# Weight sums for the last block's seven products made beside the first stages of blocks 2 to 4, with the last block's first and last group reordered

## The chip, the core and the metric

The kernel runs on one core of a Trainium2 chip. The engines work side by side, each through its own instructions in order: PE (TensorE, matmuls), PEld (the weight loads of TensorE), DVE (VectorE), ACT (ScalarE), POOL (GpSimd) and SP, which here only issues DMA transfers. The metric is the device time in microseconds (us) of one execution; lower is better.

## What is computed

Three layers over 4 x 768 = 3072 tokens of width 512, all in fp32:

```python
state = gamma * state + k_t^T v_t ; y_t = scale * q_t @ state     # retention, 8 heads of 64
xn = x / rms(x) * rms_g                                           # layer 2
x  = (silu(xn @ w_gate) * (xn @ w_val)) @ w_out                   # d_ff = 1536
h  = x @ w_in ; solu = h * softmax(h)                             # layer 3, d_ff = 1024
out = layernorm(solu) * g_ln @ w_out2
```

The weights come as doubles. Each fp32 operand of a matmul is split into a high and a low half, and a product is three matmuls: high by high, low by high, high by low.

## The kernel before

The tokens are worked in six blocks of 512 (0 to 5, `n` in the code). A block has two stages.

**First stage** (`bc_block`): layer 2 in 12 groups `m` of 128 columns of `d_ff` (`g = 12 n + m` counts them through the kernel). A group loads a gate tile and a value tile (tag `w4`, four buffers) and a tile of `w_out` (tag `wo`, two buffers), each with its halves. `gv(g, 0)` and `gv(g, 1)` are the gate and value products, 12 matmuls each into the banks GB and VB; ACT makes the Silu, `act_hl` multiplies on DVE (L613) and splits the product into halves; one group later `cmm` multiplies it by `w_out`, 12 matmuls into the banks X0 to X3. Pieces of the next block's retention (`att_pieces`) lie between: on PE the lines L154 to L185, on POOL `qd` (L144), `kd` (L136) and the state's decay (L198).

**Second stage** (`de_block`): layer 3 on four tiles `t` of 128 tokens. `d_mm` multiplies by `w_in`; DVE finds the mean (L801) and subtracts it from one half of the tile, POOL from the other half (L803); `t_tr` transposes the result on PE (L814), ACT and DVE split it (L102, L103) and `e_mm` multiplies by the second `w_out`. In the same stage `rms_1t`, `rms_2t` and `rms_3` make the next block's normalised tokens: one column sum on PE (L297), a power on POOL (L299), a transpose (L302) and four multiplications (L240, for the last block L319) on DVE. The second stage of block 0 runs behind that of block 1.

**Block 5** (`bc_block7`, since `FROM = 5`) makes the gate and value products of a group, which are two 2 x 2 products of sub-blocks, by seven half-size products instead of eight (`product(i, ...)`, 6 matmuls of 256 columns each). Products 3, 5, 6 and 7 want sums of weight sub-blocks. These are made ahead, once for each of the 12 groups: in the second stages of blocks 1, 2 and 3, four groups each (`SUMS`). `s_fetch(m)` loads a group's gate and value tiles again into the two `wo` buffers, `s_make(m)` adds the halves on POOL (L641, twice) and makes four sums (L643 to L646), and SP stores them to DRAM. In block 5 `s_load` brings a group's sums back (tag `st`, three buffers) and `s_split` makes their halves (ACT casts, L315; POOL subtracts, L316). In a group the order is products 1 and 5, the next group's split, products 6 and 7, `cm(0)` (a quarter of the group before's `w_out` product), 2 and 3, `cm(1, 2)`, product 4, `cm(3)`; at the end `cmm` does the last group's own `w_out` product.

**What sets the order.** `slot(n, s)` runs what is filed under a step `s` of block `n`, `w_slot` the weight loads of a plan: gate and value tiles are asked for two groups ahead. Up to the end of block 4 a scheduler may then move instructions on each engine; behind that (`in_order(mark)`) the order is the written one. SP issues transfers strictly in order, so a store that waits for POOL holds up the loads behind it.

Of the kernel before, what the change touches and what calls it, by code (L numbers as in the profile page):

```python
# [9 lines left out]
F32 = mybir.dt.float32  # L10
F32R = mybir.dt.float32r
# [7 lines left out]
P = 128  # L19
# [15 lines left out]
CHAIN = 12  # L35
W2_AT = [36 + 2 * j for j in range(16)]
FROM = 5
SUMS = {1: (0, 4), 2: (4, 8), 3: (8, 12)}


@with_exitstack
def retention_moe_kernel(ctx: ExitStack, tc: tile.TileContext, qk0, q2, kt, kv, wpk, w2i, w2o,
# [45 lines left out]
    def wt(tag, shape, dt, bufs):  # L88
        cnt[0] += 1
        return wp.tile(shape, dt, tag=tag, name=f"{tag}_{cnt[0]}", bufs=bufs)  # L90

    def st():
        return wt("st", [P, 512], F32, 3)
# [419 lines left out]
    def parts(w, part):  # L513

        return (w[:, :, 0, :], w[:, :, 1, :]) if part < 2 else (w[:, 0, :], w[:, 1, :])
# [74 lines left out]
    def w_slot(s):  # L590
        order = {w_split: 0, w2_fin: 0, w_conv: 1, conv: 1, w_load: 2, load64: 2}
        for f, a in sorted(wsched.pop(s, []), key=lambda x: order[x[0]]):
            f(*a)
# [6 lines left out]

    def gv(g, part):
        w = wsp.pop((g, part))
        halves = [slice(0, 256), slice(256, 512)] if g == 0 else [slice(0, 512)]
        for ts_ in halves:
            for k in range(NK):
                mm3(GV[part][:, ts_], *wk(w, k), xnh[:, k, ts_], xnl[:, k, ts_], k == 0, k == NK - 1)
# [3 lines left out]
    def act_hl(m):  # L610
        silu = acts.pop(("s", m))
        a = silu[:, 1, :]
        nc.vector.tensor_tensor(out=a, in0=GV[1], in1=silu[:, 0, :], op=ALU.mult)  # L613
        ah, al = r2(), r2()
        split(ah, al, a)
        acts[m] = (ah, al)
# [10 lines left out]
    sscr = [[dp.tile([P, 2, 256], F32, tag=f"s{m}_{i}", name=f"s{m}_{i}") for i in range(2)] for m in range(NM)]  # L627
    sums = {}

    def s_fetch(m):  # L630
        for part in range(2):
            w = wt("wo", [P, 2, 2, 256], F32R, 2)
            nc.sync.dma_start(w.bitcast(F32), scr[m][part])
            sums[m, part] = w

    def s_make(m):

        g, v = (parts(sums.pop((m, part)), part) for part in range(2))
        G = nc.gpsimd
        for hi, lo in (g, v):  # L640
            G.tensor_tensor(out=hi.bitcast(F32), in0=hi.bitcast(F32), in1=lo.bitcast(F32), op=ALU.add)  # L641
        g, v = g[0].bitcast(F32), v[0].bitcast(F32)
        G.tensor_tensor(out=v[:, 1], in0=v[:, 0], in1=v[:, 1], op=ALU.add)  # L643
        G.tensor_tensor(out=v[:, 0], in0=g[:, 0], in1=v[:, 0], op=ALU.subtract)
        G.tensor_tensor(out=g[:, 0], in0=v[:, 1], in1=g[:, 0], op=ALU.subtract)
        G.tensor_tensor(out=g[:, 1], in0=g[:, 1], in1=g[:, 0], op=ALU.subtract)  # L646
        nc.sync.dma_start(sscr[m][0], g)
        nc.sync.dma_start(sscr[m][1], v)
# [16 lines left out]
    def product(i, g, ps):  # L665

        if i in (1, 2, 4):
            w = wsp[g, 1 if i == 4 else 0]
            hi, lo = w[:, i != 1, 0, :], w[:, i != 1, 1, :]
        else:  # L670
            a, b = {6: (0, 0), 3: (0, 1), 7: (1, 0), 5: (1, 1)}[i]
            hi, lo = (t[:, a, b, :] for t in shl[g])
        xh, xl = xq(i)
        for k in range(2):
            cs = slice(k * P, k * P + P)
            mm3(ps, hi[:, cs], lo[:, cs], xh[:, k, :], xl[:, k, :], k == 0, k == 1)

    def bc_block7(n):


        base = 3 * NM * n
        V, G = nc.vector, nc.gpsimd
        gb, vb = (t.rearrange("p (h x) -> p h x", h=2) for t in GV)
        for m in range(NM):
            g = n * NM + m
            c = f4()
            cq = c.rearrange("p a (h x) -> p a h x", h=2)
            c11, c12, c21, c22 = (cq[:, a, h, :] for a in range(2) for h in range(2))
            u23 = wt("r2", [P, 2, 256], F32, 8)

            def cm(*ds):
                if m:
                    cmm(g - 1, m - 1, ds)

            def add(eng, out, x, y):
                eng.tensor_tensor(out=out, in0=x, in1=y, op=ALU.add)  # L696

            product(1, g, gb[:, 0])
            product(5, g, gb[:, 1])
            nc.scalar.copy(cq[:, :, 0, :], gb)  # L700
            if m + 1 < NM:
                s_split(g + 1)
            if m + 2 < NM:
                s_load(g + 2)
            w_slot(base + 3 * m)
            slot(n, 3 * m)
            product(6, g, vb[:, 0])
            product(7, g, vb[:, 1])
            add(V, u23[:, 0], vb[:, 0], c11)
            add(V, u23[:, 1], vb[:, 1], u23[:, 0])  # L710
            add(G, c12, u23[:, 0], c21)
            add(G, c22, u23[:, 1], c21)
            cm(0)
            product(2, g, gb[:, 0])
            product(3, g, gb[:, 1])
            slot(n, 3 * m + 1)
            w_slot(base + 3 * m + 1)
            add(V, c[:, 0, :], GV[0], c[:, 0, :])
            nc.scalar.activation(c[:, 0, :], c[:, 0, :], AF.Silu)
            if m == NM - 1 and n and PRE & 2:  # L720
                nc.scalar.activation(wt("sm", [P, 12], F32, 4)[:, 0:1], c[:, 0, 0:1], AF.Exp)
            cm(1, 2)
            product(4, g, vb[:, 0])
            add(V, c21, vb[:, 0], u23[:, 1])
            V.tensor_tensor(out=c[:, 1, :], in0=c[:, 1, :], in1=c[:, 0, :], op=ALU.mult)
            ah, al = r2(), r2()
            split(ah, al, c[:, 1, :])
            acts[m] = (ah, al)
            shl.pop(g)
            slot(n, 3 * m + 2 if m < NM - 1 else 34)  # L730
            cm(3)
            w_slot(base + 3 * m + 2)
        cmm(n * NM + NM - 1, NM - 1)

# [2 lines left out]
    def slot(n, s):  # L737
        for f in extra.pop((max(n, s // 52), s), []):
            f()

    def bc_block(n):
        base = 3 * NM * n
        for m in range(NM):
            g = n * NM + m
            if g == CHAIN:
                chain[0] = False
            with tc.issue_after(m0.ins) if g == 0 else nullcontext():
                gv(g, 0)
            s = f4()
            acts["s", m] = s  # L750
            nc.scalar.activation(s[:, 0, :], GV[0], AF.Silu)  # L751
            if m == NM - 1 and n and PRE & 2:
                nc.scalar.activation(wt("sm", [P, 12], F32, 4)[:, 0:1], s[:, 0, 0:1], AF.Exp)
            slot(n, 3 * m)
            w_slot(base + 3 * m)
            with tc.issue_after(m0.ins) if g == 0 else nullcontext():
                gv(g, 1)
            slot(n, 3 * m + 1)
            act_hl(m)
            w_slot(base + 3 * m + 1)  # L760
            if m:
                cmm(g - 1, m - 1)
            if m < NM - 1:
                slot(n, 3 * m + 2)
            else:
                slot(n, 34)
            w_slot(base + 3 * m + 2)
        cmm(n * NM + NM - 1, NM - 1)
# [247 lines left out]
    for n in range(NB):  # L1016
        if n + 1 < NB:
            if n == 0:
                span, r = 30, (31, 33, 34, 34, 35, 35)
            elif n == 1:  # L1020
                span, r = 45, (47, 49, 51, 53, 55, 57)
            else:
                span, r = 35, (37, 39, 41, 43, 45, 47) if n + 1 < FROM else (37, 39, 41, 42, 43, 44, 45, 46, 47, 48, 49, 50)
            pieces = att_pieces(n + 1)
            for i, f in enumerate(pieces):
                extra.setdefault((n, i * span // (len(pieces) - 1)), []).append(f)
            for s, f in zip(r, rms_steps(SB, n + 1)):
                extra.setdefault((n, s), []).append(f)
        if n == FROM - 1:
            g = FROM * NM  # L1030
            extra.setdefault((n, 45), []).append(lambda: s_load(g))
            extra.setdefault((n, 47), []).append(lambda: (s_split(g), s_load(g + 1)))
        if n in SUMS:
            for i, m in enumerate(range(*SUMS[n])):
                extra.setdefault((n, 36 + 4 * i), []).append(lambda m=m: s_fetch(m))
                extra.setdefault((n, 39 + 4 * i), []).append(lambda m=m: s_make(m))
        (bc_block if n < FROM else bc_block7)(n)
        if n == 0:
            after.close()
            x2_store()  # L1040
            slot(0, 35)
            continue
        de_block(n, XB, 35)
        if n == FROM - 1:
            mark = nc.cur_bb.bb.instructions[-1]
        if n == 1:
            de_block(0, x2_load(), 52)
# [72 lines left out]
```

## Time and profile before

| | |
|---|---|
| median of 3 runs | 1071.24 us (1071.00 to 1072.85) |
| the profiled execution | 1072.65 us |
| its span, first to last instruction | 1070.8 us |
| around the span | 1.85 us |
| PE busy, share of the span | 1034.8 us, 97% |
| mean granted TensorE clock | 0.986 of 2.4 GHz |

The profile is of one execution. Its own time, not the median, belongs to its rows. A matmul of 512 columns starts every 0.23 us at the full clock and every 0.43 us at half of it.

### The profile page before, as it was taken

What the parts mean: (1) busy time and instruction counts of PE and PEld (TensorE: products, weight loads), DVE (VectorE), ACT (ScalarE), POOL (GpSimd) and SP (SyncE); (2) the same over time, 40 slices, a digit from 0 to 9 for tenths busy, and PEclk for the clock granted to TensorE, in tenths of its full rate; (3) what the DMA queues carried; (4) which work ended last, traced back from release to release, by engine and by line L of the source; (5) the groups of instructions that cost most, each with busy time, mean ns of one, the idle gap of its engine ahead of it and who ended that gap; (6) DMA issues with size and microseconds to landing.
All of it is one profiled execution on the core that took longest, in us unless ns stands there. A gap on an engine that the chain in (4) does not pass through costs nothing.

```text
span 1070.8 us, 15022 instructions
## 1 busy us (share of the span) xinstructions
PE 1034.8 (97%) x5390; PEld 826.5 (77%) x5390; DVE 602.3 (56%) x1065; ACT 432.9 (40%) x816; POOL 456.7 (43%) x538
## 2 busy tenths in 40 slices
PE   9999999998999999999989999989999999999998
PEld 7867767776788777777767777767777777899887
DVE  5897877698366642353683343484244458244452
ACT  4556566456235452222353222343222236333333
POOL 6865764677147530121484010177121008455321
PEclk9899999999999999999989999998999999999999
DMA  9699998886645204666526666534665521367301
GB/s 351 203 314 336 304 316 324 272 286 215 236 157 188 99 31 160 213 196 209 178 79 205 199 211 217 189 108 138 212 212 195 171 85 30 121 235 247 108 1 40
DMA packets 73931, 203.18 MB, mean 190 GB/s; under 512 B 8321, under 2 KB 14849, under 8 KB 73857
## 3 DMA queue, kind: packets, MB, share of 16 engines
q1 hardware_dynamic: 65072, 177.05, 49.8%
q10 hardware_dynamic: 8784, 25.17, 5.9%
q8 instruction: 43, 0.70, 0.3%
q14 instruction: 32, 0.25, 0.1%
HBM read 169.68 MB, written 32.51 MB: 189 GB/s over the span
## 4 chain that ended last, share of the span: by engine, by line
PE 65%; DVE 7%; DMA 7%; POOL 6%; issue 3%; ACT 1%; SPq 0%; POOLq 0%; ACTq 0%; DVEq 0%
PE X L597 9%; PE X L598 9%; PE X L599 9%; PE GB L597 6%; PE GB L599 6%; PE GB L598 6%; PE VB L597 5%; PE VB L599 5%; PE VB L598 5%; DMA wo<-scr 4%; DVE st L502 2%; PE YB L174 2%; PE YB L171 1%; PE SB L154 1%; POOL st L501 1%
## 5 line engine op out<-in xcount | busy, mean ns | idle before, releaser
L144 POOL TENSOR_TENSOR qd<-rq,qtab_t 64x256 f32<-64x256 f32 x68 | 61.1, 899 | 189.9 <-PE YB L171 159.9
L598 PE MATMUL X<-r,wo 128*128 128x512 f32 x264 | 105.7, 400 | 0.2 <-DVE r L103 0.2
L599 PE MATMUL X<-r,wo 128*128 128x512 f32 x264 | 105.3, 399 | 0.0
L597 PE MATMUL X<-r,wo 128*128 128x512 f32 x264 | 103.1, 407 | 1.8 <-ACT r L102 1.8
L597 PE MATMUL GB<-xnh,w 128*128 128x512 f32 (+1 forms) x268 | 102.0, 380 | 2.4 <-DVE f L696 2.2
L599 PE MATMUL GB<-xnh,w 128*128 128x512 f32 (+1 forms) x268 | 100.5, 375 | 0.3 <-DVE w L103 0.3
L598 PE MATMUL GB<-xnl,w 128*128 128x512 f32 (+1 forms) x268 | 100.3, 374 | 0.0
L613 DVE TENSOR_TENSOR f<-VB,f 128x512 f32<-128x512 f32 x60 | 41.3, 689 | 95.3 <-PE VB L599 82.4
L501 POOL TENSOR_TENSOR st<-st,x 128x512 int32<-128x512 int32 x52 | 70.5, 1355 | 49.1 <-DVE st L500 18.8
L597 PE MATMUL VB<-xnh,w 128*128 128x512 f32 (+1 forms) x220 | 88.9, 404 | 0.5 <-DVE f L613 0.5
L598 PE MATMUL VB<-xnl,w 128*128 128x512 f32 (+1 forms) x220 | 86.4, 393 | 0.0
L599 PE MATMUL VB<-xnh,w 128*128 128x512 f32 (+1 forms) x220 | 86.3, 392 | 0.0
L102 ACT CAST r<-f 128x512 fp32r<-128x512 f32 x72 | 44.6, 619 | 93.1 <-DVE f L613 80.4
L103 DVE TENSOR_TENSOR r<-f,r 128x512 fp32r<-128x512 f32 x72 | 59.1, 820 | 31.5 <-ACT r L102 31.4
L502 DVE SCALAR_TENSOR_TENSOR st<-st,sq 128x512 f32<-128x512 f32 x52 | 64.0, 1230 | 22.1 <-POOL st L501 18.9
L160 DVE TENSOR_TENSOR A<-SB,s 128x256 f32<-128x256 f32 x64 | 27.0, 422 | 84.3 <-ACT s L158 84.2
L751 ACT ACTIVATE f<-GB 128x512 f32<-128x512 f32 x60 | 35.6, 593 | 94.7 <-PE GB L599 93.9
L597 PEld LDWEIGHTS GB<-xnh,w 128*128 128x128 f32 x268 | 51.0, 190 | 13.8 <-DVE f L696 2.4
L158 ACT COPY s<-SB 128x256 f32<-128x256 f32 x64 | 23.9, 374 | 93.4 <-PE SB L154 93.3
L198 POOL TENSOR_TENSOR U<-U,utab_t 64x128 f32<-64x128 f32 x52 | 25.1, 484 | 84.2 <-DVE U L196 42.2
L597 PEld LDWEIGHTS X<-r,wo 128*128 128x128 f32 x264 | 50.3, 192 | 12.7 <-ACT r L102 2.7
L599 PEld LDWEIGHTS X<-r,wo 128*128 128x128 f32 x264 | 50.4, 191 | 10.9 <-issue 0.2
(277 smaller groups left out, 2705.9 us busy)
## 6 DMA issues: line engine op xcount, KB each, us to landing
w<-scr SPq DMA_DIRECT2D x108, 512.0 KB, 3.5
wo<-scr SPq DMA_DIRECT2D x84, 512.0 KB, 3.7
x<-in_wpk SPq DMA_DIRECT2D x36, 512.0 KB, 5.1
rq<-in_q SPq DMA_DIRECT2D x40, 256.0 KB, 3.4
rv<-in_kv SPq DMA_DIRECT2D x40, 256.0 KB, 3.8
scr<-CV ACTq DMA_DIRECT2D x18, 512.0 KB, 4.5
scr<-w ACTq DMA_DIRECT2D x12, 512.0 KB, 4.5
s<-wo SPq DMA_DIRECT2D x24, 256.0 KB, 2.5
```

Source lines behind the costliest of these rows:

```text
L102: nc.scalar.copy(hi, src)
L103: (lo_eng or nc.vector).tensor_tensor(out=lo, in0=src, in1=hi.bitcast(F32), op=ALU.subtract)
L144: nc.gpsimd.tensor_tensor(out=qd[r], in0=tq4[r, :, hh, :], in1=qtab_t[r, 2 * u:2 * u + 2, :], op=ALU.mult)
L160: nc.vector.tensor_tensor(out=A, in0=s4[:, :, 0, :], in1=s2, op=ALU.add)
L198: nc.gpsimd.tensor_tensor(out=new, in0=old, in1=utab_t[r, ps].unsqueeze(2).to_broadcast([64, ps.stop - ps.start, 64]), op=ALU.mult)
L501: nc.gpsimd.tensor_tensor(out=ti, in0=ti, in1=lo, op=ALU.add)
L502: lastc[0] = nc.vector.scalar_tensor_tensor(out=t, in0=t, scalar=3.4028234663852886e38, in1=g, op0=ALU.min, op1=ALU.mult)
L597: nc.tensor.matmul(ps, lhsT=lh, rhs=rh, start=start, stop=False)
L598: nc.tensor.matmul(ps, lhsT=lh, rhs=rl, start=False, stop=False)
L599: nc.tensor.matmul(ps, lhsT=ll, rhs=rh, start=False, stop=stop)
L613: nc.vector.tensor_tensor(out=a, in0=GV[1], in1=silu[:, 0, :], op=ALU.mult)
L751: nc.scalar.activation(s[:, 0, :], GV[0], AF.Silu)
```

## The change

The sums move from the second stages of blocks 1 to 3 into the first stages of blocks 2, 3 and 4. There `gv` has a group's gate and value tiles in SBUF anyway: in every third group (`m % 3 == n % 3`) `s_sum` adds the halves of each on POOL into an `st` buffer (two buffers a group), and behind `act_hl` `s_make` makes the four sums in place and stores them as before. The second loads (`s_fetch`, 24 transfers of 512 KB) go. Because `st` buffers are now in use up to block 4, the first loads of sums come later.

In block 5's first group nothing is split any more: group 61's split moves into the end of block 4's second stage, behind group 60's (steps 46 and 48 instead of 47). In the last group all seven products come first, and behind them the four quarters of the group before's `w_out` product, `cm(0)` to `cm(3)`.

```diff
-SUMS = {1: (0, 4), 2: (4, 8), 3: (8, 12)}
+SUMS = (2, 3, 4)
...
     def gv(g, part):
         w = wsp.pop((g, part))
+        n, m = divmod(g, NM)
+        if n in SUMS and m % 3 == n % 3:
+            s_sum(part, w)
...
-    def s_fetch(m):
-        for part in range(2):
-            w = wt("wo", [P, 2, 2, 256], F32R, 2)
-            nc.sync.dma_start(w.bitcast(F32), scr[m][part])
-            sums[m, part] = w
+    def s_sum(part, w):
+        hi, lo = parts(w, part)
+        sums[part] = t = st().rearrange("p (h x) -> p h x", h=2)
+        nc.gpsimd.tensor_tensor(out=t, in0=hi.bitcast(F32), in1=lo.bitcast(F32), op=ALU.add)
 
     def s_make(m):
-
-        g, v = (parts(sums.pop((m, part)), part) for part in range(2))
+        g, v = sums.pop(0), sums.pop(1)
         G = nc.gpsimd
-        for hi, lo in (g, v):
-            G.tensor_tensor(out=hi.bitcast(F32), in0=hi.bitcast(F32), in1=lo.bitcast(F32), op=ALU.add)
-        g, v = g[0].bitcast(F32), v[0].bitcast(F32)
...
-            if m + 1 < NM:
+            if 0 < m < NM - 1:
                 s_split(g + 1)
...
-            cm(0)
+            if m < NM - 1:
+                cm(0)
             product(2, g, gb[:, 0])
             product(3, g, gb[:, 1])
+            last = m == NM - 1
+            if last:
+                product(4, g, vb[:, 0])
...
-            cm(1, 2)
-            product(4, g, vb[:, 0])
+            if not last:
+                cm(1, 2)
+                product(4, g, vb[:, 0])
...
-            cm(3)
+            cm(*range(0 if last else 3, NK))
...
             act_hl(m)
+            if 0 in sums:
+                s_make(m)
...
-            extra.setdefault((n, 47), []).append(lambda: (s_split(g), s_load(g + 1)))
-        if n in SUMS:
-            for i, m in enumerate(range(*SUMS[n])):
-                extra.setdefault((n, 36 + 4 * i), []).append(lambda m=m: s_fetch(m))
-                extra.setdefault((n, 39 + 4 * i), []).append(lambda m=m: s_make(m))
+            extra.setdefault((n, 46), []).append(lambda: (s_split(g), s_load(g + 1)))
+            extra.setdefault((n, 48), []).append(lambda: s_split(g + 1))
```

Where this moves instructions, in program order (line numbers of the changed kernel are a few higher: L803 becomes L808, L823 L828, L696 L694, L641 L636, L643 to L646 L641 to L644).

POOL before, around the middle of block 2's second stage; `f_701` is tile 0 of the stage, `rsum` the norm of block 3, `wo_...` the tiles of two groups whose sums are made:

```order
L641 TENSOR_TENSOR wo_4712<-wo_4712 128x2x256
L641 TENSOR_TENSOR wo_4714<-wo_4714 128x2x256
L198 TENSOR_TENSOR U_80<-U_79,utab_t 64x2x64 x2
L643 TENSOR_TENSOR wo_4714<-wo_4714 128x256
L823 TENSOR_TENSOR sm_4609<-sm_4609 128x1
L136 TENSOR_TENSOR kd_5058<-rv_4579,ktab_t 128x256
L803 TENSOR_SCALAR f_701_4611<-f_701_4611,sm_4609 128x512
L644 TENSOR_TENSOR wo_4714<-wo_4712,wo_4714 128x256
L645 TENSOR_TENSOR wo_4712<-wo_4714,wo_4712 128x256
L823 TENSOR_TENSOR sm_4653<-sm_4653 128x1
L646 TENSOR_TENSOR wo_4712<-wo_4712 128x256
L299 TENSOR_TENSOR rsum<-rsum,mhalf 128x16
```

and the same place in the changed kernel, with tile 0 as `f_699`:

```order
L198 TENSOR_TENSOR U_80<-U_79,utab_t 64x2x64 x2
L828 TENSOR_TENSOR sm_4597<-sm_4597 128x1
L136 TENSOR_TENSOR kd_5006<-rv_4571,ktab_t 128x256
L808 TENSOR_SCALAR f_699_4599<-f_699_4599,sm_4597 128x512
L828 TENSOR_TENSOR sm_4641<-sm_4641 128x1
L829 TENSOR_TENSOR sm_4597<-sm_4597 128x1
L830 TENSOR_SCALAR sm_4597<-sm_4597 128x1
L299 TENSOR_TENSOR rsum<-rsum,mhalf 128x16
```

The sums are gone from between the retention's work, the tile's subtraction and the power of the norm.

POOL in the changed kernel, in block 2's first stage at the group whose gate and value tiles are `w_579` and `w_585`:

```order
L136 TENSOR_TENSOR kd_3853<-rv_3773,ktab_t 128x256
L636 TENSOR_TENSOR st_3950<-w_579_3875 128x512
L636 TENSOR_TENSOR st_3991<-w_585_3910 128x512
L641 TENSOR_TENSOR st_3991<-st_3991 128x256
L642 TENSOR_TENSOR st_3991<-st_3950,st_3991 128x256
L643 TENSOR_TENSOR st_3950<-st_3991,st_3950 128x256
L144 TENSOR_TENSOR qd_3984<-rq_3902,qtab_t 64x256 x2
L644 TENSOR_TENSOR st_3950<-st_3950 128x256
L198 TENSOR_TENSOR U_80<-U_79,utab_t 64x2x64 x2
```

In the kernel before only the rows of `kd`, `qd` and `U` stand there; six sum instructions have come between them.

PE at block 5's last group before, from the last matmul of `cm(1, 2)` on (`wo_8557` is the `w_out` tile of the group before, `wo_8630` that of the last group):

```order
L599 MATMUL X_70<-r_1253_8608,wo_8557 128x512
L597 MATMUL VB<-kst_7679,w_1252_8559 128x256
L598 MATMUL VB<-kst_7680,w_1252_8559 128x256
L599 MATMUL VB<-kst_7679,w_1252_8559 128x256
L597 MATMUL VB<-kst_7679,w_1252_8559 128x256
L598 MATMUL VB<-kst_7680,w_1252_8559 128x256
L599 MATMUL VB<-kst_7679,w_1252_8559 128x256
L597 MATMUL X_71<-r_1253_8608,wo_8557 128x512
L598 MATMUL X_71<-r_1254_8609,wo_8557 128x512
L599 MATMUL X_71<-r_1253_8608,wo_8557 128x512
L597 MATMUL X_68<-r_1259_8681,wo_8630 128x512
```

and after, from the last matmul of product 3 on:

```order
L599 MATMUL GB<-xnh,x_1250_8528 128x256
L597 MATMUL VB<-kst_7661,w_1252_8535 128x256
L598 MATMUL VB<-kst_7662,w_1252_8535 128x256
L599 MATMUL VB<-kst_7661,w_1252_8535 128x256
L597 MATMUL VB<-kst_7661,w_1252_8535 128x256
L598 MATMUL VB<-kst_7662,w_1252_8535 128x256
L599 MATMUL VB<-kst_7661,w_1252_8535 128x256
L597 MATMUL X_68<-r_1253_8584,wo_8533 128x512
L598 MATMUL X_68<-r_1254_8585,wo_8533 128x512
...
L599 MATMUL X_71<-r_1253_8584,wo_8533 128x512
L597 MATMUL X_68<-r_1259_8648,wo_8606 128x512
```

Product 4 (VB) has moved ahead of all twelve matmuls with the group before's tile, of which only three stood behind it.

## Rows read from the trace of the kernel before

**Rows 1.** page, part 1: busy us, share of the span, number of instructions, per engine

```profile
PE 1034.8 (97%) x5390; PEld 826.5 (77%) x5390; DVE 602.3 (56%) x1065; ACT 432.9 (40%) x816; POOL 456.7 (43%) x538
```

**Rows 2.** windows: a first-stage stretch and a second-stage stretch of block 2; busy us per engine

```profile
417.00:517.00 100.00, 100.00 (x515) 78.62 (x514) 43.28 (x71) 28.06 (x52) 16.95 (x27) 1.00 0.61 202
...
520.00:562.00 42.00, 37.60 (x180) 29.64 (x179) 33.83 (x69) 18.69 (x40) 32.22 (x37) 0.92 0.32 108
```

**Rows 3.** timeline of PE, second stages: start us, us, line, tile; idle before, releaser

```profile
349.57 0.66 PE L814 MATMUL X<-ident,f 128*128 128x128 f32 x4 [1.21 <-POOL f L803]
...
542.79 1.11 PE L814 MATMUL VB<-ident,f 128*128 128x128 f32 x4 [3.14 <-POOL f L803]
...
544.98 0.63 PE L599 MATMUL GB<-w2oh,r 128*128 128x512 f32 x1
...
548.39 0.39 PE L598 MATMUL GB<-w2ol,r 128*128 128x512 f32 x1
...
561.53 0.50 PE L597 MATMUL X<-w2oh,r 128*128 128x512 f32 x1 [1.06 <-DVE r L103]
...
723.69 0.79 PE L599 MATMUL GB<-w2oh,r 128*128 128x512 f32 x1 [3.89 <-DVE r L103]
...
729.35 0.40 PE L597 MATMUL VB<-w2ih,x 128*128 128x512 f32 x1
```

**Rows 4.** timeline of POOL in second stages of blocks 2 and 3

```profile
537.37 1.28 POOL L641 TENSOR_TENSOR wo<-wo 128x512 f32<-128x512 f32 x1 [1.95 <-DMA wo<-scr]
...
714.44 2.93 POOL L299 TENSOR_TENSOR rsum<-rsum,mhalf 128x16 f32<-128x16 f32 x1
```

**Rows 5.** timeline of DVE in second stages of blocks 2, 3 and 4

```profile
541.86 0.67 DVE L103 TENSOR_TENSOR r<-GB,r 128x512 fp32r<-128x512 f32 x1
...
550.49 4.80 DVE L240 SCALAR_TENSOR_TENSOR xT<-xT,rg_t,ssq 128x512 f32<-128x512 f32 x4
...
717.41 0.71 DVE L302 STREAM_TRANSPOSE ssq<-rsum 128x512 f32<-128x512 f32 x1 [2.13 <-POOL rsum L299]
...
718.63 3.67 DVE L240 SCALAR_TENSOR_TENSOR xT<-xT,rg_t,ssq 128x512 f32<-128x512 f32 x4
...
890.83 2.74 DVE L319 SCALAR_TENSOR_TENSOR xT<-xT,rg_t,ssq 128x512 f32<-128x512 f32 x4
```

**Rows 6.** groups of POOL: count, then busy us, mean ns of one, idle before

```profile
L641 POOL TENSOR_TENSOR wo<-wo 128x512 f32<-128x512 f32 x24 | 33.4, 1392 | 42.7 <-DMA wo<-scr 42.5
...
L646 POOL TENSOR_TENSOR wo<-wo 128x256 f32<-128x256 f32 x12 | 9.4, 780 | 0.6
```

**Rows 7.** timelines of PE, POOL and DVE at the start of block 5

```profile
928.04 0.39 PE L597 MATMUL GB<-xnh,w 128*128 128x256 f32 x1 [2.18 <-DVE f L696]
...
924.05 2.52 POOL L316 TENSOR_TENSOR x<-st,x 128x512 fp32r<-128x512 f32 x2 [6.93 <-ACT x L315]
...
927.29 0.69 DVE L696 TENSOR_TENSOR f<-GB,f 128x512 f32<-128x512 f32 x1 [2.67 <-POOL f L696]
```

**Rows 8.** timelines of PE and ACT at block 5's last group

```profile
1014.45 0.50 PE L597 MATMUL X<-r,wo 128*128 128x512 f32 x1 [1.39 <-ACT r L102]
...
1019.36 0.42 PE L597 MATMUL GB<-w2ih,x 128*128 128x512 f32 x1
...
1011.75 1.28 ACT L721 ACT_TABLE_LOAD   x1
```

**Rows 9.** timelines of DVE and PE in block 2's first stage; loads there

```profile
474.27 0.69 DVE L613 TENSOR_TENSOR f<-VB,f 128x512 f32<-128x512 f32 x1 [3.85 <-PE VB L599]
...
481.52 0.48 PE L597 MATMUL VB<-xnh,w 128*128 128x512 f32 x1
...
w<-scr SPq DMA_DIRECT2D x21, 512.0 KB, 3.4
```

**Rows 10.** timelines of POOL and PE in block 4's second stage

```profile
909.26 1.85 POOL L803 TENSOR_SCALAR f<-f,sm 128x512 f32<-128x512 f32 x1 [0.77 <-DVE sm L801]
...
913.40 0.60 PE L814 MATMUL X<-ident,f 128*128 128x128 f32 x4
```

## The prediction

> **What bounds the kernel.** I read the page's first part first: PE is busy 97% of the span, DVE 56%, ACT 40%, POOL 43% [rows 1]. So a gain must shorten a wait of PE, or a stretch in which PE runs at half rate. The windows next: in a first stage PE has work all of the time (100 us of 100) and POOL is busy only 17; in a second stage PE is busy 37.6 of 42, POOL 32 and DVE 34, and the granted clock is 0.92 [rows 2]. POOL is thus short of time exactly where the sums lie, and idle where they go to. Last the timeline of PE, for the waits themselves and what ended each.
>
> In block 1 PE waits 1.21 us and in block 2 3.14 for POOL's half of L803; in block 3 it waits 3.89 for a split on DVE [rows 3]. At the start of block 5 it waits 2.18 and at its end 1.39 [rows 7, 8]. After the three longest of block 2, block 3 and the block's end the matmuls start 0.43 us apart instead of 0.23 for a while, which is the 1.2 GHz level in place of 2.4; behind the 2.18 they do not. All this is about 22 us; the start of the kernel (blocks 0 and 1 up to the latter's second stage) keeps its orders.
>
> The profiled execution took 1072.65 us, 1.85 of it around the span, and the median is 1071.24, so 1.4 less: the sum is made against the former and carried to the latter. A measurement of this kernel can tell about 0.2%, some 2 us, from no change.
>
> **T1, block 1.** What PE waits for is POOL's half of L803, and POOL comes to it late because sums and waits for reloaded tiles stand ahead of it (the groups' idle time before L641 is 42.7 us in all, nearly all of it for those loads [rows 6]). Without them PE has no reason to wait: 1.2 us; 0.6 if DVE's half is nearly as late.
>
> **T2, block 2.** Ahead of L803 POOL waited 1.95 us for a reloaded tile and then added its halves for 1.28, the first of two [rows 4]; with the other sums some 4 us. With POOL free, the next late one is DVE: its split of GB (L103) ends at 541.86 + 0.67 = 542.53 [rows 5], and what stands ahead of it on DVE is slowed by POOL at its side, by 0.8 us as an estimate (less than half of the 2.06 that four multiplications lose further down). Then the matmuls that now start at 544.98 start at about 541.8: 3.2 us. From 544.98 to 548.39 eight intervals take 3.41 us, at 0.23 they would take 1.84, so 1.5 us come back if PE no longer falls to half rate. The wait of 1.06 at 561.53 is for DVE, which in this stretch has four multiplications of 4.80 us together beside the sums; in block 4, with no sums beside, the same four take 2.74 [rows 3, 5]. I take 0.8 of that wait. Sum 5.5; if the clock falls all the same and the 1.06 stays, 3.2; at most 6.2.
>
> **T3, block 3.** The chain is column sum, POOL's power (L299, 714.44 to 717.37), DVE's transpose (L302, idle 2.13 for it), multiplications, and the split that PE waits for at 723.69 [rows 3 to 5]. The power stands behind a sum and an L803 that came late; of the 2.13 I take 1.5 as an estimate (the two, 0.8 and 0.7). The four multiplications lose 0.9 beside POOL (3.67 from 718.63, against 2.74 in block 4 [rows 5]). Of these 2.4 us I take 2.2, since POOL's own L803 now stands there too. The 13 intervals from 723.69 to 729.35 take 5.66 us against 3.03 at 0.23; PE still has a wait of some 1.7 us there, and behind waits of 3 us the rate fell, behind 2.18 it did not, so I count half of the 2.6: 1.3. Sum 3.5; ends 2.2 and 4.8.
>
> By the Trainium skill ("SBUF — State Buffer", SBUF: two separate sides) DVE and POOL share a pair of ports that one instruction holds alone, where the DVE instruction reads both operands from SBUF. The trace agrees in direction, with the 4.80 beside POOL and the 2.74 without.
>
> **T4, start of block 5.** POOL begins the split of group 61 at 924.05 (2.52 us), and only then its additions, of which DVE's at 927.29 wants the first, and PE that one [rows 7]. Without the split POOL's addition, some 0.7 us, starts at about 924.2 behind DVE's, DVE's at 925.25, and PE's product at 926.0 instead of 928.04: 2.0 us. PE can get no more than its 2.18; I keep 1.5 below, for ACT's copy.
>
> **T5, end of block 5.** Product 4 comes nine matmuls of 0.23 earlier relative to the end of the group, so PE has these 2.1 us of work while DVE and ACT finish. But ACT loads the Exp table (1.28 us from 1011.75) before the cast that PE waits for [rows 8]. Silu and load move 0.7 us up with product 3, which stands behind one quarter of `cm` less: the load ends at 1012.33, a small Exp and the cast take 0.8 as an estimate, and PE starts at about 1013.2 instead of 1014.45. Its second matmul, on the low half, comes at 1013.95 in place of 1015.17. So 1.25 us; the eight intervals from 1015.98 to 1019.36 take 3.38 against 1.87, 1.5 more if the rate stays. Sum 2.75; ends 1.2 and 3.2.
>
> **What is added.** Six sum instructions in every third group, 2 x 1.39 + 4 x 0.78 = 5.9 us [rows 6], twelve times, the same count as before. A group has at least 36 matmuls of 0.23, 8.3 us, and POOL is 83% idle there: nothing on the path, with these covers. (a) What stands behind the sums on POOL is `qd` and the state's decay, used by PE a group or more later; 5.9 us would be paid in full only if they were used at once. (b) DVE's L613 frees VB at 474.96 and PE wants VB at 481.52 [rows 9]: 6.5 us cover. (c) The tiles are now also read by POOL, and SP's stores wait for POOL with loads behind them. A load is asked for when PE has left the buffer and lands 3.4 us later [rows 9]; its next use is two groups on, 2 x 8.3 - 2.8 (the product itself) - 3.4 = 10.4 us cover, against 5.9 of work. (d) Group 61's split stands in block 4's second stage: one subtraction of some 1.3 us ahead of the last tile's L803, which may end at 911.6 or a little later instead of 911.1; PE transposes that half at 913.40 [rows 10]. Cover 2.3 us; beyond it each us costs one. (e) The 24 loads that go free DMA time in the second stages (0.32 busy [rows 2]); no wait of PE named them directly, so nothing.
>
> **Sum.** 1.2 + 5.5 + 3.5 + 2.0 + 2.75 = 14.95. 1072.65 - 14.95 = 1057.7 for an execution like the profiled one; 1056.3 from the median; I say 1057. All low ends: 0.6 + 3.2 + 2.2 + 1.5 + 1.2 = 8.7, so 1062.5 to 1064. All high ends: 1.2 + 6.2 + 4.8 + 2.2 + 3.2 = 17.6, so 1053.6 to 1055.
>
> **Rivals.**
>
> *A: the waits shrink but the rate still falls, or DVE is late soon after.* DVE has 34 us of work in 42 [rows 2], and the terms T2, T3 and T5 hold 4.3 us of full rate that depend on waits being short enough. Against it: the waits left are under 2 us, and behind 2.18 the rate held. It gives the low ends, 8 to 9 us: 1063. Chance 0.25.
>
> *B: the loads of the first stages come late (the other side).* SP issues in order, so each store of sums holds the gate, value and `w_out` loads behind it until POOL has finished. The place is the group after next in blocks 2 to 4, twelve times. It costs nothing up to the 10.4 us; at 11.6 (14.95 / 12 = 1.25 more) it has eaten the gain, and at 12 it makes 12 x 1.6 - 15 = 4 us over, 1075. For it: POOL must also take `kd`, which itself waits for loaded data, ahead of the sums. Against it: the work is 5.9 us and POOL is idle 83% of that stage. Chance 0.06.
>
> *C: POOL beside DVE in the first stages.* Sums that slow DVE as the multiplications of 4.80 were slowed cost up to 5.9 us in a group, where L613 has 6.5. Beyond 6.5 PE waits for VB; at 7.7 it is 15 us in twelve groups, and the time is the old one, 1071. For it: the ratio of 4.80 to 2.74. Against it: DVE is busy only 43% there [rows 2]. Chance 0.06.
>
> By the page named above the lock would hold only DVE instructions with both operands in SBUF, and L613 reads VB; by that page C is weaker than I price it, and no run here shows it yet.
>
> **Numbers.** The forecast has 0.63, A 0.25, B 0.06, C 0.06. The range 1053 to 1066 takes in the forecast with its bounds and A, and leaves out B and C. Faster by over 0.2%: 0.63 + 0.25 = 0.88; same: C, 0.06; slower: B, 0.06.
>
> **What would show it.** In the changed kernel's timeline: PE's waits for L803 in blocks 1 and 2 gone, with the wait in block 2 at most 0.5 us and on DVE; the wait before block 3's split 1.7 us or less, and no more than half of the slow matmuls behind it; the wait at block 5's start under 0.4; that at its end under 0.7 in two pieces, behind ACT. First stages of blocks 2 to 4 still with PE at 100 of 100 us and POOL up from 17 to some 35. POOL's power in block 3 starting at the DVE sum. The prediction is wrong if PE waits in these first stages for a tile of weights (B) or for DVE's L613 (C), if the waits stay in the second stages under another name, or if the matmuls behind them still start 0.43 us apart (A).

## The result, and the profile after

| | before | changed |
|---|---|---|
| median | 1071.12 us (1070.83 to 1072.85, 4 runs) | 1055.11 us (1054.95 to 1055.25, 4 runs) |
| span of the profiled execution | 1070.8 us | 1053.3 us |
| mean granted TensorE clock there | 0.986 | 0.995 |

The ratio is 0.9847, 95% interval 0.983 to 0.9864: 16.4 us less, between 14.6 and 18.2. The two profiled executions are 17.5 us apart. In the experiments some executions of most kernels have a lower mean clock and take longer from their first 50 us on; where that moves a median, the executions with a clock of 0.99 or more are named.

The page's first part of the changed kernel answers to [rows 1]. PE's busy time fell by 9.7 us though it has the same 5390 matmuls; some 6 us of that are the 29 matmuls at half rate that the last section counts in the trace of before, 0.2 us each.

```profile
PE 1025.1 (97%) x5390; PEld 820.2 (78%) x5390; DVE 601.7 (57%) x1065; ACT 432.9 (41%) x816; POOL 458.4 (44%) x538
```

The same windows as in [rows 2], the second moved with the kernel (us of PE, PEld, DVE, ACT and POOL busy, then granted clock, DMA share, GB/s):

```profile
417.00:517.00 100.00, 100.00 (x516) 78.60 (x515) 49.01 (x70) 27.99 (x53) 41.20 (x52) 1.00 0.68 224
...
518.00:554.00 36.00, 34.20 (x177) 27.16 (x176) 28.55 (x68) 16.32 (x37) 17.97 (x22) 1.00 0.18 60
```

In the first stage PE still works 100 of 100 us, with POOL at 41 in place of 17. In the second stage PE idles 1.8 us of 36 in place of 4.4 of 42, the clock is 1.00 in place of 0.92, POOL has 18 us in place of 32.

PE's timeline, at the places of [rows 3], [rows 7] and [rows 8]:

```profile
348.19 0.60 PE L819 MATMUL X<-ident,f 128*128 128x128 f32 x4
...
538.80 0.40 PE L297 MATMUL SB<-rsum,sel_t 128*128 128x16 f32 x2 [0.84 <-DVE rsum L296]
...
540.13 0.50 PE L597 MATMUL GB<-w2oh,r 128*128 128x512 f32 x1 [0.93 <-DVE r L103]
...
540.70 0.39 PE L599 MATMUL GB<-w2oh,r 128*128 128x512 f32 x1
...
542.55 0.39 PE L598 MATMUL GB<-w2ol,r 128*128 128x512 f32 x1
...
713.48 0.50 PE L599 MATMUL GB<-w2oh,r 128*128 128x512 f32 x1 [1.78 <-DVE r L103]
...
716.61 0.40 PE L597 MATMUL VB<-w2ih,x 128*128 128x512 f32 x1
...
913.41 0.39 PE L597 MATMUL GB<-xnh,w 128*128 128x256 f32 x1 [0.15 <-DVE f L694]
...
998.45 0.49 PE L597 MATMUL X<-r,wo 128*128 128x512 f32 x1
...
999.17 0.50 PE L598 MATMUL X<-r,wo 128*128 128x512 f32 x1 [0.23 <-DVE r L103]
...
1001.84 0.39 PE L597 MATMUL GB<-w2ih,x 128*128 128x512 f32 x1
```

The matmul that began at 349.57, 544.98, 548.39, 723.69, 729.35, 928.04, 1014.45 and 1019.36 [rows 3, 7, 8] now begins at 348.19, 540.70, 542.55, 713.48, 716.61, 913.41, 998.45 and 1001.84. The differences are 1.4, 4.3, 5.8, 10.2, 12.7, 14.6, 16.0 and 17.5 us. The first is T1 (less 0.2 that the changed kernel's trace had lost by then), the next two lie in T2, 10.2 and 12.7 in T3, 14.6 is T4, and the last two are T5. What T1 and T2 gain between these places is in the table further down. POOL no longer releases any of PE's waits shown here; in block 2 and in block 3 it is DVE.

The timelines of POOL, DVE and ACT at the places of [rows 4, 5, 7, 8, 10] show what stands behind that:

```profile
704.74 2.94 POOL L299 TENSOR_TENSOR rsum<-rsum,mhalf 128x16 f32<-128x16 f32 x1 [1.20 <-DVE sm L806]
...
895.47 1.31 POOL L316 TENSOR_TENSOR x<-st,x 128x512 fp32r<-128x512 f32 x1
...
911.52 1.44 POOL L694 TENSOR_TENSOR f<-r,f 128x256 f32<-128x256 f32 x2 [6.64 <-DVE r L694]
```

```profile
539.41 0.67 DVE L103 TENSOR_TENSOR r<-GB,r 128x512 fp32r<-128x512 f32 x1
...
544.38 2.72 DVE L240 SCALAR_TENSOR_TENSOR xT<-xT,rg_t,ssq 128x512 f32<-128x512 f32 x4
...
707.72 0.71 DVE L302 STREAM_TRANSPOSE ssq<-rsum 128x512 f32<-128x512 f32 x1
...
709.35 2.75 DVE L240 SCALAR_TENSOR_TENSOR xT<-xT,rg_t,ssq 128x512 f32<-128x512 f32 x4
...
712.74 0.68 DVE L103 TENSOR_TENSOR r<-VB,r 128x512 fp32r<-128x512 f32 x1
```

```profile
996.39 1.28 ACT L723 ACT_TABLE_LOAD   x1
...
997.79 0.60 ACT L102 CAST r<-f 128x512 fp32r<-128x512 f32 x1
```

POOL's power (L299) now waits 1.20 us for DVE instead of standing behind sums, DVE's transpose L302 follows without an idle time, its four multiplications take 2.72 and 2.75 us in place of 4.80 and 3.67, and the split at 712.74 is still behind them. In block 5's first group the additions of POOL start at 911.52 right behind DVE's. Half of group 61's split stands at 895.47 ahead of the last tile's L803 (L808 here, at 897.10), and PE has no wait there. At the end the table load runs from 996.39 to 997.67, and the cast starts at 997.79.

### The profile page after: what moved, and what is told of

It reads as the page before. It is cut to its first block, busy times and chain, and to the rows that moved or that the text cites. A ratio compares the mean times of both kernels' runs of the same rounds, so it can differ in the third digit from the quotient of the medians.

```text
span 1053.3 us, 14997 instructions
## 1 busy us (share of the span) xinstructions
PE 1025.1 (97%) x5390; PEld 820.2 (78%) x5390; DVE 601.7 (57%) x1065; ACT 432.9 (41%) x816; POOL 458.4 (44%) x538
## 4 chain that ended last, share of the span: by engine, by line
PE 74%; DVE 8%; POOL 2%; ACT 2%; issue 2%; DMA 2%; SPq 0%; POOLq 0%; ACTq 0%; DVEq 0%
PE X L597 10%; PE X L598 10%; PE X L599 10%; PE GB L597 6%; PE GB L599 6%; PE GB L598 6%; PE VB L597 6%; PE VB L599 6%; PE VB L598 6%; DVE st L502 3%; PE YB L174 2%; POOL st L501 2%; PE YB L171 1%; PE SB L154 1%; PE X L819 1%
## 5 line engine op out<-in xcount | busy, mean ns | idle before, releaser
L598 PE MATMUL X<-r,wo 128*128 128x512 f32 x264 | 104.3, 395 | 0.2 <-DVE r L103 0.2
L599 PE MATMUL X<-r,wo 128*128 128x512 f32 x264 | 104.0, 394 | 0.0
L597 PE MATMUL X<-r,wo 128*128 128x512 f32 x264 | 101.9, 402 | 0.5 <-ACT r L102 0.4
L616 DVE TENSOR_TENSOR f<-VB,f 128x512 f32<-128x512 f32 x60 | 41.3, 689 | 94.5 <-PE VB L599 70.4
L103 DVE TENSOR_TENSOR r<-f,r 128x512 fp32r<-128x512 f32 x72 | 63.3, 879 | 31.7 <-ACT r L102 31.6
L636 POOL TENSOR_TENSOR st<-w 128x512 f32<-128x512 f32 x24 | 31.4, 1308 | 72.9 <-DMA w<-scr 72.6
L597 PEld LDWEIGHTS GB<-xnh,w 128*128 128x128 f32 x268 | 50.9, 190 | 11.7 <-issue 0.9
L599 PEld LDWEIGHTS GB<-xnh,w 128*128 128x128 f32 x268 | 50.9, 190 | 9.9 <-DVE w L103 0.9
L598 PEld LDWEIGHTS GB<-xnl,w 128*128 128x128 f32 x268 | 50.9, 190 | 9.5 <-issue 0.3
```

The lines of the kernel that those rows point to most:

```text
L103: (lo_eng or nc.vector).tensor_tensor(out=lo, in0=src, in1=hi.bitcast(F32), op=ALU.subtract)
L597: nc.tensor.matmul(ps, lhsT=lh, rhs=rh, start=start, stop=False)
L598: nc.tensor.matmul(ps, lhsT=lh, rhs=rl, start=False, stop=False)
L599: nc.tensor.matmul(ps, lhsT=ll, rhs=rh, start=False, stop=stop)
L636: nc.gpsimd.tensor_tensor(out=t, in0=hi.bitcast(F32), in1=lo.bitcast(F32), op=ALU.add)
```

## The experiments

In these runs the kernel before took 1068.4 to 1076.6 us in most executions, so the place of a matmul in the traces tells more here than a median. "The shift" is the start of a matmul less that of the same matmul in the first trace of the kernel named.

**Only the sums moved.** The changed kernel with the old block 5:

```diff
-            if 0 < m < NM - 1:
+            if m + 1 < NM:
                 s_split(g + 1)
...
-            extra.setdefault((n, 46), []).append(lambda: (s_split(g), s_load(g + 1)))
-            extra.setdefault((n, 48), []).append(lambda: s_split(g + 1))
+            extra.setdefault((n, 47), []).append(lambda: (s_split(g), s_load(g + 1)))
```

and the last group's products in their old places.

> The sums are moved, block 5's two edits are undone. Theory (the terms add, and each sits where the waits were): the waits in the second stages of blocks 1 to 3 shrink as in the changed kernel, those of 2.2 us at block 5's start and 1.4 us at its end stay. 16.0 us of the whole less the 1.9 and 2.9 that the changed kernel's trace gives for block 5: about 11 us faster than before, 1060. Rival (the moved loads, not the edits in block 5, brought part of T4 and T5): 13 us or more, 1058 or less.

Ratio 0.992 (0.9874 to 0.9966). The median is 1071.25; the four executions with a clock of 0.99 or more took 1060.1 to 1061.7 (the kernel before at such clocks: 1068.9 to 1071.3). The profiled one was 14.4 us behind by its 50th us, ahead of any edit. From there the shift against the kernel before falls by 2.2 us up to block 2's second stage, 3.9 in it and 5.3 in block 3's, and by nothing in block 5, where PE waits 2.14 and 1.39 us as before. The slow matmuls of block 2 are still there, so the 3.9 are without them. That is 11.4 in all, so the theory holds and the rival falls.

**Only the split**, in the kernel before, the same lines the other way round.

> The kernel before, with group 61's split in block 4's second stage. Theory: PE's wait of 2.18 us at block 5's start goes, nothing else moves: 1.5 to 2.2 us faster, 1069. Rival (the split delays the last tile's L803 in block 4, whose cover is 2.3 us): below 1 us, with a new wait of PE behind block 4's last transposes.

Ratio 0.9946 (0.9911 to 0.998), which is 2 to 10 us: too wide to tell 1.5 to 2.2. In the trace PE's wait at block 5's start is gone, and the shift goes from 0.0 to -1.9 there; block 4's transposes wait for nothing new, so the rival falls. PE's timeline at block 5's end:

```profile
1012.54 0.50 PE L597 MATMUL X<-r,wo 128*128 128x512 f32 x1 [1.39 <-ACT r L102]
```

The 1.39 us at the end are there as in [rows 8], but the matmuls behind them run at full rate, 1.6 us less without an edit; in blocks 1 and 2 the shift moves by up to 0.8 in the same way.

**Only the last group**, in the kernel before:

```diff
...
+            last = m == NM - 1
+            if last:
+                product(4, g, vb[:, 0])
...
-            cm(3)
+            cm(*range(0 if last else 3, NK))
```

> The kernel before, with block 5's last group in the new order. Theory: the waits of 1.39 and 0.22 us shrink to 0.3 or less and the eight slow intervals behind them run at full rate: 2.5 to 3 us faster, 1068.3. Rival A (the Exp table load holds the cast, the rate still falls): 1.2 us or less.

Ratio 0.9948 (0.9916 to 0.998). The shift goes from -2.46 to -5.41 at this place, 2.95 us; the wait on ACT is gone and 0.22 us on the low half is left (PE's timeline):

```profile
1011.35 0.50 PE L598 MATMUL X<-r,wo 128*128 128x512 f32 x1 [0.22 <-DVE r L103]
```

Of the 2.95 some 1.5 are the slow matmuls, and the run above gained as much without this edit. Over all traces they stand behind the old order's waits in three of five, and in none of eight with the new order.

**Sums without the second loads**, the kernel before with

```diff
     def s_fetch(m):
-        for part in range(2):
-            w = wt("wo", [P, 2, 2, 256], F32R, 2)
-            nc.sync.dma_start(w.bitcast(F32), scr[m][part])
-            sums[m, part] = w
+        pass
```

and the halves of `x2h` and `x2l` added in `s_make` into `st` buffers.

> The kernel before, with the sums in the second stages as there, but of tiles that are in SBUF already (halves of layer 3's input), so that the 24 loads go and POOL waits for none; the sums are of other data than the reference's, the amount of work is the same. Theory that POOL's wait for reloaded tiles is the larger share of what makes L803 late (42.5 us idle in all before L641, 1.95 just ahead of the wait in block 2): 5 to 9 us faster, 1064. Rival that POOL's own work in the second stage does it: 0 to 3 us faster, and PE still waits for POOL's L803 in block 2.

1065.71 against 1073.34, ratio 0.9931 (0.9893 to 0.9969): 7.6 us, in the theory's range. PE in blocks 2, 4 and 5:

```profile
538.97 0.60 PE L811 MATMUL VB<-ident,f 128*128 128x128 f32 x4
...
542.20 0.50 PE L597 MATMUL GB<-w2oh,r 128*128 128x512 f32 x1 [1.40 <-DVE r L103]
...
882.95 0.50 PE L597 MATMUL GB<-w2oh,r 128*128 128x512 f32 x1 [3.36 <-DVE r L103]
...
922.89 0.41 PE L599 MATMUL VB<-qhl,x 128*128 128x256 f32 x1
923.11 0.41 PE L597 MATMUL VB<-qhl,x 128*128 128x256 f32 x1
```

The transposes at 538.97 have no wait for POOL, with all of POOL's work still in this stage. Up to the end of block 3 the shift falls by 8.7 us, where it fell by 11.4 with only the sums moved: the loads that POOL waited for were the larger share. The 2.7 left go with POOL's own work or with the other order that the scheduler gave DVE and PE here; this run does not part the two. In block 4, where nothing was edited, that order makes PE wait 3.36 us and costs 0.5 of the gain. At block 5's start PE waits 2.13 us, and from 1.4 us later 13 matmuls of 256 columns start 0.21 us apart in place of 0.12: 1.5 us lost. At block 5's end the slow matmuls are missing, which gives 1.6 back.

**The loads put back** into the changed kernel, read by nobody:

```diff
...
+        if 1 <= n <= 3:
+            for i, m in enumerate(range(4 * n - 4, 4 * n)):
+                extra.setdefault((n, 36 + 4 * i), []).append(lambda m=m: s_fetch(m))
```

> The changed kernel with the 24 loads of 512 KB put back into the second stages of blocks 1 to 3, into the same buffers; nobody reads them. Theory (the loads cost only because POOL waited for them, not by their traffic): within 1 us of the changed kernel, 1055, and PE's waits in the second stages as there. Rival (the traffic or SP's queue was part of the gain): 2 us or more slower than the changed kernel, with a wait of PE for a weight tile at the start of blocks 2 to 4.

1061.58 (the profiled one 1061.4), 6.5 us over the changed kernel. In blocks 2 and 3 PE's waits are 0.84, 0.93 and 1.78 as in the changed kernel, as the theory says; 1.5 us of the difference are slow matmuls in block 2. In block 1 the theory fails, and the wait is not the one that the rival named. PE's, POOL's and SP's timelines, and the load of `rv` in 300 to 330 us (count, size, us from issue to landing):

```profile
325.27 0.66 PE L824 MATMUL X<-ident,f 128*128 128x128 f32 x4 [2.89 <-POOL f L813]
```

```profile
322.90 0.61 POOL L136 TENSOR_TENSOR kd<-rv,ktab_t 128x256 f32<-128x256 f32 x1 [6.81 <-DVE sm L801]
```

```profile
299.04 8.48 SPq L641 DMA_DIRECT2D wo<-scr  x4
...
308.42 6.77 SPq L641 DMA_DIRECT2D wo<-scr  x4
...
318.04 0.43 SPq L115 DMA_DIRECT2D rv<-in_kv  x1
```

```profile
rv<-in_kv SPq DMA_DIRECT2D x1, 256.0 KB, 4.8
```

Since no reader held them back, SP sent the eight loads of block 1 one behind another, and the load of `rv` left at 318.04 instead of 314.67 and took 4.8 us to land instead of 3.4. POOL's `kd` (L136) reads it. Its row names DVE's L801 as the releaser, which had ended 7 us before; in the changed kernel the row of the same `kd` names the load of `rv`. Behind `kd` on POOL stands L803 (L813 here), for which PE waits: 4.7 us with the slow matmuls behind. So the loads cost PE nothing in blocks 2 and 3; in block 1 they stand in SP's queue ahead of a load that is wanted (3.4 us), and beside them its landing takes 1.4 us longer.

**32 sets of sums in place of 12**:

```diff
-        if n in SUMS and m % 3 == n % 3:
+        if n in SUMS and (m % 3 == n % 3 or m > 1):
```

> The changed kernel with 32 sets of sums in the first stages of blocks 2 to 4 in place of 12 (every group from the third on; each set is made again with the same values). Theory (POOL is idle in 59 us of 100 there, and the covers of 6.5 and 10.4 us hold): PE busy 100 of 100 us still, within 1 us of the changed kernel, POOL near 75 of 100. Rival C (POOL at DVE's side makes DVE late for VB) or B (SP's stores hold the loads): PE waits of 0.3 us or more in most groups, 6 us or more slower than the changed kernel.

1066.35, the profiled one with a span of 1061.7: at this load the theory fails, with POOL at 64 of 100. Block 3's first stage by windows, PE's waits in it and in block 4, and SP's queue ahead of the first:

```profile
589.00:689.00 100.00, 96.69 (x482) 75.90 (x481) 44.69 (x67) 27.63 (x52) 64.29 (x72) 0.99 0.72 249
```

```profile
687.73 2.04 PE L597 MATMUL X<-r,wo 128*128 128x512 f32 x4 [3.31 <-DMA wo<-scr]
...
860.69 1.17 PE L597 MATMUL X<-r,wo 128*128 128x512 f32 x4 [1.38 <-DMA wo<-scr]
```

```profile
670.74 0.40 SPq L529 DMA_DIRECT2D w<-scr  x1
...
677.47 0.32 SPq L646 DMA_DIRECT2D s<-st  x1
...
681.02 0.38 SPq L529 DMA_DIRECT2D wo<-scr  x1
```

PE waits for a tile of `w_out`, twice. SP stood at a store from 671.1 to 677.5, until POOL had made the sum, and the load for PE left at 681.02. That is rival B's mechanism, at 2.7 times the work, in two places and not in most groups: the first wait and the slow matmuls behind it cost 6.2 us, the second wait 1.6. PE has no wait of 0.2 us or more for DVE in these first stages: no sign of C.

**Two multiplications on POOL**, in the changed kernel:

```diff
+        if bank is ssq and k > 1:
+            nc.gpsimd.tensor_tensor(out=xT[:, k, :], in0=xT[:, k, :], in1=bank, op=ALU.mult)
+            nc.gpsimd.tensor_scalar(xT[:, k, :], xT[:, k, :], rg_t[:, k:k + 1], None, ALU.mult)
...
```

> The changed kernel, in which two of the four multiplications of the norm in the second stages of blocks 1 to 3 (L240) go to POOL, as a product and a scaling each. Theory (after the change DVE is late next in block 3: the 2.75 us of these four stand ahead of the split that PE waits 1.78 us for): that wait falls by about 1.4 us, to 0.4, and the kernel is 1 to 1.5 us faster than the changed one, 1054. Rival (DVE's place is taken by POOL's L808, which now stands behind two products): no gain, a wait for POOL there.

1059.32; the wait of 1.78 is 1.49, and a new one of 3.36 stands in block 4, where the order changed as above. The theory misses. The rival's "no gain" came, but not by a wait for POOL. DVE in block 3:

```profile
709.99 2.45 DVE L244 SCALAR_TENSOR_TENSOR xT<-xT,rg_t,ssq 128x512 f32<-128x512 f32 x2
...
713.10 0.68 DVE L103 TENSOR_TENSOR r<-VB,r 128x512 fp32r<-128x512 f32 x1
```

The two that stayed take 2.45 us beside POOL's product (L241, two of 3.43 us together from 710.15), nearly what four took without it, so the split came hardly earlier.

**The kernel before, once more.**

> The kernel before, once more. It asks which of the slow stretches of matmuls come back in another execution. If the rate follows the wait ahead of it, the stretches behind 3.14, 3.89 and 1.39 us of waiting are all there; if not, the waits stay and some stretches go, 1.5 us each in block 2 and at block 5's end.

Span 1069.4. The waits of 3.14, 3.90, 2.19 and 1.39 us are there and so are the three slow stretches, but shorter: block 1's wait is 0.43 instead of 1.21, and the slow matmuls are 5, 8 and 7 instead of 9, 12 and 8 (the last section has the table).

**The changed kernel once more, a change to it, and no sums.**

> The changed kernel once more, beside the next two. Theory: PE's waits are those of its first trace (0.84 and 0.93 us in block 2, 1.78 in block 3, 1.05 in block 4, none over 0.3 in block 5); its time is 12 to 17 us below that of the kernel before on the same chip, and what moves between executions is stretches of matmuls at half rate.

1056.73 against 1073.06, ratio 0.9866 (0.9828 to 0.9904); the waits are the same to 0.01 us. In its trace PE runs at half rate behind the 0.93, as the changed kernel did not at first (PE, block 2):

```profile
540.48 0.50 PE L597 MATMUL GB<-w2oh,r 128*128 128x512 f32 x1 [0.93 <-DVE r L103]
...
541.75 0.63 PE L599 MATMUL GB<-w2oh,r 128*128 128x512 f32 x1
```

For the next one, the norm's four multiplications go behind the split:

```diff
     def rms_2t(n=0):
+        if n > 2:
+            lo = lnst[0][0][1][1]
+            nc.vector.scalar_tensor_tensor(out=rsum[:, 0:1], in0=lo[:, 0:1].bitcast(F32), scalar=0.0,
+                                           in1=rsum[:, 0:1], op0=ALU.mult, op1=ALU.add)
```

and `rms_2t` goes from step 39 to 41.

> The changed kernel, in which the norm's transpose and four multiplications wait on DVE for the split of tile 0 (in the second stages of blocks 2 to 4 a one-column instruction of DVE reads that split, times zero, ahead of the transpose). Theory (DVE's multiplications ahead of the split are what is late next): PE's waits of 1.78 and 1.05 us go to 0.3 or less, 2 to 2.5 us faster than the changed kernel. Rival (the split is late for ACT's cast or for the norm's own chain, and the next block's first products wait for the norm in turn): less than 1 us, with a new wait of PE at the start of blocks 4 or 5.

1053.52, ratio 0.9822 (0.9799 to 0.9844): 3.2 us below the changed kernel just above and the fastest version here. But 1.5 of the 3.5 us between these two traces are block 2's slow stretch. Against the first trace of the changed kernel, which has none either, the shift falls by 2.1 us, within the theory's 2 to 2.5. DVE in block 3, PE in blocks 3 and 5:

```profile
710.39 0.68 DVE L103 TENSOR_TENSOR r<-VB,r 128x512 fp32r<-128x512 f32 x1
...
714.10 2.73 DVE L240 SCALAR_TENSOR_TENSOR xT<-xT,rg_t,ssq 128x512 f32<-128x512 f32 x4
```

```profile
711.70 0.48 PE L603 MATMUL GB<-w2oh,r 128*128 128x512 f32 x1
...
909.20 0.38 PE L601 MATMUL GB<-xnh,w 128*128 128x256 f32 x1 [1.30 <-ACT f L702]
```

The split is at 710.39, ahead of the multiplications; the third matmul at 711.70 has no wait, where it had 1.78. In block 4 the 1.05 goes as well, but the new wait of the rival is there: 1.30 us at block 5's start, behind ACT.

> The changed kernel with no sums at all: the high halves of the gate and value tiles are stored in their place, so POOL's 74 instructions go and block 5's seven products are of other data. Theory (the sums beside the first stages cost nothing): as the changed kernel within 1 us. Rival C (POOL slows DVE there to PE's cost): faster than the changed kernel by 2 us or more.

1056.61, ratio 0.9869 (0.9822 to 0.9916). POOL has 72 instructions less, not 74. PE's waits are those of the changed kernel; from 60 us to the end the shift against its first trace stays between 0.7 and 1.1 us. Its window of block 2's first stage:

```profile
417.00:517.00 100.00, 100.00 (x515) 78.62 (x514) 43.01 (x71) 28.07 (x52) 17.06 (x27) 1.00 0.70 224
```

PE has 100 of 100 us with or without the sums: they cost nothing there.

## Why the prediction held, term by term

The forecast was 1057 with 14.95 us less; the traces gave 17.5 and the medians 16.0.

| term | forecast | between the two traces | what the experiments add |
|---|---|---|---|
| T1, block 1 | 1.2 | 1.6, and 0.6 where a retention product has another place on PE | before's wait here is 0.4 to 1.2, by execution |
| T2, block 2 | 5.5 | 5.5 | 3.9 where the half rate stays (only the sums) |
| T3, block 3 | 3.5 | 5.3 | 5.3 |
| T4, block 5's start | 2.0 | 1.9 | 1.9 |
| T5, block 5's end | 2.75 | 2.9 | 2.95 |
| added work | 0 | 0 | 0 (no sums) |

(The changed kernel's trace had lost 0.2 us by block 1.)

**The one mis-sized term is T3.** The step was "I count half of the 2.6": the slow matmuls behind block 3's split are all gone, 2.5 us, though PE still waits 1.78. The other part, up to the split, is 2.8 in place of 2.2: DVE's multiplications lose nothing beside POOL now, and a wait of 0.30 ahead went too. What is left of the wait is DVE's split behind L240, as the run that moves L240 shows.

**T2** has its size by parts that missed both ways. The next late one was DVE's split as forecast, 539.41 to 540.08, but PE waits 0.84 for DVE's column sum ahead of it and 0.93 for it, not "at most 0.5": up to the third matmul it is 2.3 in place of 3.2. The slow stretch gave 1.6 (1.5), and what follows 1.6 in place of 0.8.

**T5** assumed PE would still wait 0.3 us for ACT; the cast began at 997.79 and PE at 998.45 with no wait that the profile reports. The order of cast and table load is as forecast. Of its 2.9 us, 1.5 are the rate, which two of five traces with the old order don't lose either.

**The median moved less than the traces**: the first profiled execution of before had all three slow stretches, with 29 slow matmuls, and that of the changed kernel none of them. That fits with the repeat, which has 20 and a span 1.4 us shorter, but the executions behind the median have no trace.

**Two numbers of the prediction don't come out of its rows.** "About 22 us" for the waits and the slow matmuls is 17.4 (11.8 of waits, 5.6 of half rate), and no term uses it. T2's high end of 6.2 would be 5.8 (3.2 + 1.5 + 1.06), so the high ends add up to 17.2 in place of 17.6.

**Rivals.** A did not come about in this trace, but the same waits in block 2 gave it in three of the seven other traces with them, 1.5 us each. The argument against A, that waits under 2 us are left and the rate held behind 2.18, was weak: in the same trace the rate fell behind 1.39 [rows 8]. So T2's 1.5 us of full rate was in part luck. B is real as a mechanism and came about at 2.7 times the work; where it begins was not measured. For C, the group of POOL's larger sums in the changed kernel (count, busy us, mean ns, idle before):

```profile
L636 POOL TENSOR_TENSOR st<-w 128x512 f32<-128x512 f32 x24 | 31.4, 1308 | 72.9 <-DMA w<-scr 72.6
```

With the four smaller ones, of 0.78 us on average, a set takes 2 x 1.31 + 4 x 0.78 = 5.7 us, against 5.9 forecast. POOL reads 41 us in the window instead of "some 35" because that window holds four sets. What that does to DVE is in its group of L613, of before and then of the changed kernel (L616), and in the timelines of DVE and POOL in block 2's first stage after the change:

```profile
L613 DVE TENSOR_TENSOR f<-VB,f 128x512 f32<-128x512 f32 x60 | 41.3, 689 | 95.3 <-PE VB L599 82.4 <-issue 8.3 <-ACT f L751 4.0
```

```profile
L616 DVE TENSOR_TENSOR f<-VB,f 128x512 f32<-128x512 f32 x60 | 41.3, 689 | 94.5 <-PE VB L599 70.4 <-PE SB L154 11.3 <-issue 8.2
```

```profile
501.76 0.69 DVE L616 TENSOR_TENSOR f<-VB,f 128x512 f32<-128x512 f32 x1 [2.34 <-PE VB L599]
...
503.16 1.78 DVE L103 TENSOR_TENSOR r<-f,r 128x512 fp32r<-128x512 f32 x1
```

```profile
501.78 0.74 POOL L644 TENSOR_TENSOR st<-st 128x256 f32<-128x256 f32 x1
...
503.03 1.37 POOL L636 TENSOR_TENSOR st<-w 128x512 f32<-128x512 f32 x1 [0.51 <-DMA w<-scr]
```

L613, now L616, which reads VB, takes 689 ns in both kernels, and 0.69 us at 501.76 with a sum of POOL at its side. The split (L103), with both operands in SBUF, takes 0.69 us at 512.73 with no sum beside it, but 1.78 at 503.16: it ends 0.54 us behind POOL's sum, which began before it. Its mean over the kernel goes from 820 to 879 ns, since few splits meet a sum. DVE's busy time in the window rises from 43.3 to 49.0 us, 1.4 for each set, and PE doesn't see it behind 6.5 us of cover. The Trainium skill ("SBUF — State Buffer", SBUF: two separate sides) separates the two kinds as these rows do, and has the one that starts later wait for the whole of the other; the 1.78 us agree with that.

## What to carry to other kernels

Work that a slow engine does for later belongs beside a stage in which the bounding engine never waits, and best where its operands lie in SBUF already: the second loads made up 8.7 of the 11.4 us that moving the sums gained. Price such a move by the row of what is late next, not by the whole wait; then price its limit, which here was a store in an in-order queue ahead of a load (at 2.7 times the work) and not the engine itself. And before a stall is given a price, look whether the matmuls behind it run at half rate: those us are real, but they come and go between executions.

## What the runs showed of the hardware

Matmuls of 512 columns that start 0.43 us apart, the 1.2 GHz level, were counted behind the waits of each trace:

| PE's wait ahead | traces | matmuls at half rate |
|---|---|---|
| 2.87 to 3.15, block 2 (before's order) | 4 | 9, 8, 6, 5 |
| 3.89 to 3.90, block 3 (before's order) | 4 | 12, 11, 14, 8 |
| 3.36, block 4 (no second loads; two multiplications on POOL) | 2 | 0, 7 |
| 1.39 and 0.22, block 5's end (before's order) | 5 | 8, 0, 7, 0, 7 |
| 2.13 to 2.19, block 5's start (before's order) | 5 | 0 in four; in one 1, and 13 of 256 columns 0.21 us apart |
| 1.49 to 1.78, block 3 (changed order) | 7 | 0 in all |
| 0.84 and 0.93, block 2 (changed order) | 8 | 0 in five, 7 in three |
| 0.84 and 1.40, block 2 (no second loads) | 1 | 7 |
| 2.89, block 1 (loads put back) | 1 | 7 |
| 3.31 and 1.38, first stages of blocks 3 and 4 (32 sets) | 1 | 12 and 0 |
| 1.30, block 5's start (norm behind the split) | 1 | 0 |

Single waits of 1.49 to 1.78 us in block 3 kept 2.4 GHz all seven times, those of 2.13 to 2.19 four times in five, and one of 3.36 once in two, while two of 0.84 and 0.93 us close together lost it three times in eight. Length alone doesn't decide it, and what else does is not settled here.
